# Routing attention and an ELU layer on one core: the steps of the ordering placed one by one between the products

## The chip, the cores and the metric

One Trainium2 chip, one core. The metric is the device time of one execution in microseconds. The kernel before was timed three times, with a median of 1534.33 us (1527.32 to 1535.45). "Third" below is a unit of work, explained with the kernel.

## The reference

Attention in which a query only sees the keys of its own cluster, then two matrix products with an ELU between them:

```python
def _attn_ref(q, k, v, centroids):            # q, k, v: (4, 8, 768, 64); centroids: (8, 16, 64)
    ...
    q_assign = np.argmax(np.einsum('bhsd,hcd->bhsc', q_n, c_n), axis=-1)
    k_assign = np.argmax(np.einsum('bhsd,hcd->bhsc', k_n, c_n), axis=-1)
    mask = q_assign[:, :, :, None] == k_assign[:, :, None, :]
    scores = scale * np.matmul(q, k.transpose(0, 1, 3, 2))
    scores = np.where(mask, scores, -1000000000.0)
    ...
    return np.matmul(attn, v).astype(np.float32)

def _moe_ref(x, w_in, w_out):                 # x: (3072, 512); w_in: (512, 2048); w_out: (2048, 512)
    h = x @ w_in
    g = np.where(h > 0.0, h, alpha * (np.exp(np.minimum(h, 0.0)) - 1.0))
    return (g @ w_out).astype(np.float32)
```

The weights come as 8-byte floats, and the kernel turns them into 4-byte ones itself.

## The kernel before, in words

Two heads are a pair; each of the four batches has four pairs, numbered 0 to 15 through all of them. The rows of x are cut into twelve **thirds** of 256 rows, three to a batch. The products of one third are twelve steps: four `hidden` steps (32 matmuls L780 each, then the ELU on ScalarE and VectorE) and eight `outer` steps (L804, 8 rows of the trace each, the first four into `o_bank`, the others into `f_bank`).

**Batch 0** is done densely, in eight blocks: `scores` (L446, L455, exp on ScalarE), `values` (L471, the reciprocal L482 on VectorE, the multiply L485 on GpSimd). Between them `weigh` converts the weights, 32 pieces of 512 KB of words: VectorE L306 to L315, ScalarE L301 and L302, and at the end a multiply on GpSimd (L318). After each piece `ask` loads the next words into the place that came free (L291). Sixteen pieces wait in the buffer of `w_out`, which is filled last.

**Batches 1 to 3** don't compute all scores. `ready(b)` is a list of 19 steps that order the rows by clusters: `load_plain` (SP), `turn_plain` (VectorE L365), `clusters` (TensorE L372), `running` (VectorE, `cum` L509), `starts` (TensorE L520), `ranks` (TensorE L535 and L543, VectorE `idx` L550), `limits`. With `idx` known, each pair is copied in DRAM into the order of its clusters, in two parts: `load_rows` loads a part (six DMAs on SP, L577, into `rows`, which has two buffers), `scatter` writes it out (12 indirect DMAs on GpSimd, L595). `load_sorted` (SP, L146 and L613) reads the pair back once both parts have landed. `turn_sorted` and `near_masks` (VectorE L620 to L630) prepare it; `attend` computes scores against the neighbouring tiles only (`near_scores`, L645 and L654) and the values of the pair before (`near_values`, L697 and L709, reciprocal L724). `store_x` writes the result on ScalarE's queue, `gather` fetches the 256 rows of a third (16 indirect DMAs on GpSimd, L749, for nine thirds), and `turn_x` transposes them for the products.

Everything is written out by hand: the order in which these functions are called is the order on each engine and each queue. Before, a table `beside` puts the steps of third 0 beside blocks 4 to 7, with three steps of `ready(1)` in each block. Then, for each batch, all four pairs are scattered at once:

```python
    def spread(i):
        for part in range(2):
            scatter(i, part)
            if i % NPR + 1 < NPR:
                load_rows(i + 1, part)
...
    for i in range(NPR, 2 * NPR):
        spread(i)
    load_sorted(NPR)
```

and a table `plans` says for each batch behind which product step a pair is attended and a third is gathered. The next batch's four pairs follow in one lump at the end of the batch.

Of the kernel before, what the change touches and what calls it, by code (L numbers as in the profile page):

```python
# [63 lines left out]
def main_path(ctx, tc, c, q, k, v, centroids, moe_w_in, moe_w_out, out):  # L64
# [39 lines left out]
    def take(n):  # L104
        nonlocal used
        used += n
        return spare[:, used - n : used]
# [169 lines left out]
    def ask():  # L277

        nonlocal asked
        while asked < len(pieces):  # L280
            to, src = pieces[asked]
            if not wide:
                nc.sync.dma_start(to, src)
                asked += 1
                continue
            places[:] = [x for x in places if asked < x[1]]
            if not places:
                return
            place, limit = places.pop(0)
            w = place.bitcast(U32)  # L290
            nc.sync.dma_start(w, src.bitcast(U32))  # L291
            words[asked] = (w.rearrange("p (n w) -> p n w", w=2), place, limit)
            asked += 1

# [30 lines left out]
    while used + 2 * WC <= FC * DM:  # L325
        limit = into + used // DM - 1
        places.append((take(2 * WC), limit))
    ask()
    rest = weight_steps()

    def weigh(n):
        for _ in range(n):
            next(rest, None)
# [220 lines left out]
    def limits(b):  # L554

        end = ends[b]
        for j in range(2):
            nc.vector.tensor_tensor(
                reach[:, 2 * (b - 1) + j : 2 * (b - 1) + j + 1],
                end[:, 2 * j + 1 : 2 * j + 2],  # L560
                end[:, 2 - 2 * j : 3 - 2 * j],
                op=Alu.subtract,
            )
        both = ends[b] = route.tile([P, 2, 4], F32, name="both", tag="both", bufs=2)
        for to in range(2):
# [17 lines left out]

    def scatter(i, part):
        b, pr = pairs[i]
        if part == 0:
            for e in range(2):
                q_in[i, e] = dram.tile([S, D], F32, name=f"q_in_{i}_{e}")
                kv_in[i, e] = dram.tile([S, 2 * D], F32, name=f"kv_in_{i}_{e}")
        rows = nat.pop((i, part))  # L590
        for t in range(HT):
            for j, to, cols in ((0, q_in, slice(0, D)), (1, kv_in, slice(D, 3 * D))):
                for e in range(2):
                    at = (part * HT + t) * H + 2 * pr + e
# [224 lines left out]
    def product_steps(third):  # L819
        return [lambda n=n: hidden(third, n) for n in range(FC // 4)] + [  # L820
            lambda t=t, part=part: outer(third, t, part) for t in range(2) for part in range(4)
        ]


    def ready(b):

        some = ((0, 1), (2, 3))
        load = lambda j, n: lambda: [load_plain(b, j, pr) for pr in some[n]]
        turn = lambda j, n: lambda: [turn_plain(b, j, pr) for pr in some[n]]
        return [load(0, 0), turn(0, 0), load(0, 1), turn(0, 1)] + [  # L830
            lambda: clusters(b, 0, 0),
            lambda: clusters(b, 0, 1),
            load(1, 0),
            lambda: running(b, 0),
            lambda: starts(b, 0),
            turn(1, 0),
            load(1, 1),
            lambda: ranks(b, 0),
            turn(1, 1),
            lambda: clusters(b, 1, 0),  # L840
            lambda: clusters(b, 1, 1),
            lambda: running(b, 1),
            lambda: starts(b, 1),
            lambda: ranks(b, 1),
            lambda: [limits(b)] + [load_rows(b * NPR, part) for part in range(2)],
        ]

    def spread(i):
        for part in range(2):
            scatter(i, part)  # L850
            if i % NPR + 1 < NPR:
                load_rows(i + 1, part)

    def attend(i):

# [12 lines left out]
        if j == 0:  # L868
            masks(0)

    todo = product_steps(0)
    beside = {4: [0, 1], 5: [2, 3], 6: [4, 5, 6, 7], 7: [8, 9, 10, 11]}
    first = ready(1)
    for n in range(len(blocks)):
        if n > 0:
            values(n - 1)
        if n + 1 < len(blocks):
            v_of[n + 1] = load_v(blocks[n + 1][1])
        scores(n)
        if n > 0:  # L880
            check(n - 1, n - 1)
        if n + 1 < len(blocks):
            masks(n + 1)
        weigh(4 if n < 4 else 0)
        for m in beside.get(n, []):
            todo[m]()
            weigh(4)
        if n >= 1:
            for step in first[3 * n - 3 : 3 * n]:
                step()  # L890
    values(len(blocks) - 1)
    check(len(blocks) - 1, len(blocks) - 1)

    plans = {
        1: {"attend": (0, 2, 4, 8), "last": 12, "ready": 8, "gather": 18},
        2: {"attend": (8, 16, 22, 28), "last": 32, "ready": 0, "gather": 34},
        3: {"attend": (4, 10, 16, 22), "last": 26, "ready": None, "gather": 30},
        4: {"attend": (), "last": None, "ready": None, "gather": None},  # L900
    }
    for i in range(NPR, 2 * NPR):
        spread(i)
    load_sorted(NPR)
    for b, plan in plans.items():
        thirds = range(3 * b - 2 if b == 1 else 3 * b - 3, 3 * b)
        todo = [step for third in thirds for step in product_steps(third)]
        events = {}

        def at(m, *what):  # L910
            events.setdefault(m, []).extend(what)

        for n, m in enumerate(plan["attend"]):
            i = b * NPR + n
            at(m - 1, lambda i=i: [turn_sorted(i), near_masks(i)])
            at(m, lambda i=i: attend(i))
            if n + 1 < NPR:
                at(m, lambda i=i: load_sorted(i + 1))
            if n > 0:
                at(m + 2, lambda i=i: store_x(i - 1))  # L920
        if plan["last"] is not None:
            i = (b + 1) * NPR - 1
            at(plan["last"], lambda i=i: [near_values(i), check(i, NPR + i)])
            at(plan["last"] + 2, lambda i=i: store_x(i))
            at(plan["gather"], lambda b=b: gather(3 * b))
            at(len(todo), lambda b=b: turn_x(3 * b))
        if b > 1:
            at(0, lambda b=b: gather(3 * b - 2))
            at(11, lambda b=b: turn_x(3 * b - 2))
            at(12, lambda b=b: gather(3 * b - 1))  # L930
            at(23, lambda b=b: turn_x(3 * b - 1))
        if plan["ready"] is not None:
            steps = ready(b + 1)
            for n, step in enumerate(steps):
                at(min(plan["ready"] + n + 1, len(todo)), step)
        for m in sorted(set(events) | set(range(len(todo)))):
            for event in events.get(m, []):
                event()
            if 0 <= m < len(todo):
                todo[m]()  # L940
        if plan["ready"] is not None:
            for i in range((b + 1) * NPR, (b + 2) * NPR):
                spread(i)
            load_sorted((b + 1) * NPR)


    ok = c["ok"]
# [238 lines left out]
```

## Time and profile before

| | |
|---|---|
| median of three runs | 1534.33 us |
| profiled execution | 1534.54 us |
| its span | 1532.8 us |
| TensorE busy | 1010.3 us (66%) |
| VectorE busy | 413.4 us (27%) |
| ScalarE busy | 323.5 us (21%) |
| GpSimd busy | 475.1 us (31%) |
| mean granted clock of TensorE | 0.81 |
| chain that ended last: TensorE | 55% |
| chain: "issue" | 19% |
| chain: another core or an unknown queue | 11% |

The span is cut into 40 slices on the page, and the digits there are tenths of a slice in which the engine was busy. "issue" in the chain and as the reason of an idle stretch means that the engine waited for nothing that the profile shows. In the lists of waits a line gives the engine and its line, what it waited for, the microseconds in total, how often, and the longest.

### The profile page before, as it was taken

The page shows a single profiled execution, that of the slowest core. Times are in us where ns is not written, and L with a number is a line of the kernel's source. Part 1 is how long each engine was busy: PE and PEld are TensorE (multiplying, and loading weights), DVE is VectorE, ACT ScalarE, POOL GpSimd, SP SyncE. Part 2 cuts the span into 40 slices and gives each one's busy share as a digit, 9 for nine tenths or more (in the row PEclk, how much of TensorE's full clock was granted, in tenths as well). Part 3 has the DMA queues.
Part 4 walks back from the last instruction along what each step waited for, and adds up shares of the span by engine and source line. Part 5 has one row for each costly group of instructions (what it writes and reads, how often), then busy time and mean ns, then how long its engine had stood idle before and what let it go on. Part 6 is the DMA issues. An engine that isn't in the chain of part 4 may idle for free.

```text
span 1532.8 us, 11444 instructions
## 1 busy us (share of the span) xinstructions
PE 1010.3 (66%) x4259; PEld 592.6 (39%) x4259; DVE 413.4 (27%) x618; ACT 323.5 (21%) x488; POOL 475.1 (31%) x494
## 2 busy tenths in 40 slices
PE   7547438800189998222399999522229999959998
PEld 4215223300065565100047474310114746545774
DVE  4553534100155632001044534000012444100100
ACT  5643342200033310000023232000002324111220
POOL 1222221077710034777300000777740000450000
PEclk9878679955599999555589999755559999979999
DMA  7623321022523342234411411223400220110000
GB/s 217 155 67 85 86 69 48 7 68 70 131 40 70 62 76 62 77 84 89 66 28 28 87 36 30 57 74 85 90 15 7 50 50 20 33 28 14 0 14 16
DMA packets 296206, 91.60 MB, mean 60 GB/s; under 512 B 278992, under 2 KB 282064, under 8 KB 296144
## 3 DMA queue, kind: packets, MB, share of 16 engines
q1 hardware_dynamic: 241232, 60.88, 18.3%
q0 software_dynamic: 13824, 18.90, 4.3%
q10 hardware_dynamic: 41088, 11.01, 2.9%
q8 instruction: 36, 0.59, 0.2%
q14 instruction: 26, 0.21, 0.0%
HBM read 65.57 MB, written 25.17 MB: 59 GB/s over the span
## 4 chain that ended last, share of the span: by engine, by line
PE 55%; issue 19%; another core or an unknown queue 11%; DVE 7%; ACT 4%; POOL 2%; DMA 1%; SPq 0%; ACTq 0%; DVEq 0%; POOLq 0%
PE banks L780 20%; PE o_bank L804 11%; PE f_bank L804 9%; PE banks L471 4%; PE banks L697 3%; PE banks L645 2%; PE banks L372 2%; PE banks L709 1%; DVE ex L312 1%; DVE r L724 1%; POOL w_in L318 1%; ACT p L662 1%; DVE r L482 1%; PE banks L446 1%
## 5 line engine op out<-in xcount | busy, mean ns | idle before, releaser
L780 PE MATMUL banks<-xT,w_in 128*128 128x256 f32 x1536 | 382.1, 399 | 243.8 <-issue 221.7
L780 PEld LDWEIGHTS banks<-xT,w_in 128*128 128x128 f32 x1536 | 305.5, 200 | 320.6 <-issue 258.3
L749 POOL DMA_INDIRECT rows_x<-x_in,idx x144 | 138.8, 964 | 535.9 <-DMA x_in<-back 491.5
L804 PE MATMUL o_bank<-w_out,gT 128*128 128x512 f32 x384 | 176.4, 613 | 16.0 <-issue 16.0
L795 DVE SCALAR_TENSOR_TENSOR gT<-gT,banks 128x1024 f32<-128x1024 f32 x48 | 58.2, 1213 | 469.2 <-ACT gT L792 372.2
L804 PE MATMUL f_bank<-w_out,gT 128*128 128x512 f32 x384 | 171.5, 600 | 0.0
L791 ACT ACTIVATE gT<-banks 128x1024 f32<-128x1024 f32 x48 | 49.1, 1024 | 545.7 <-remote 215.9
L595 POOL DMA_INDIRECT kv_in<-rows,idx x144 | 139.1, 966 | 58.1 <-issue 43.6
L595 POOL DMA_INDIRECT q_in<-rows,idx x144 | 138.8, 964 | 57.6 <-issue 45.2
L645 PE MATMUL banks<-qT,kT 64*128 64x384 f32 (+1 forms) x288 | 58.0, 483 | 116.8 <-issue 110.2
L804 PEld LDWEIGHTS o_bank<-w_out,gT 128*128 128x128 f32 x384 | 74.1, 195 | 110.3 <-issue 109.1
L804 PEld LDWEIGHTS f_bank<-w_out,gT 128*128 128x128 f32 x384 | 72.2, 191 | 88.7 <-issue 88.7
L724 DVE RECIPROCAL r<-r 128x384 f32<-128x384 f32 x24 | 61.2, 2549 | 127.2 <-ACT r L723 118.0
L662 ACT ACTIVATE p<-banks 128x768 f32<-128x768 f32 (+1 forms) x72 | 52.5, 740 | 130.3 <-issue 110.1
L645 PEld LDWEIGHTS banks<-qT,kT 64*128 64x128 f32 x288 | 24.1, 191 | 142.3 <-issue 121.0
L372 PE MATMUL banks<-plain,cT 128*32 128x384 f32 x96 | 25.0, 624 | 68.4 <-DVE plain L365 52.6
L365 DVE STREAM_TRANSPOSE plain<-blk 128x768 f32<-128x768 f32 x24 | 22.4, 960 | 146.1 <-issue 112.5
L792 ACT ACTIVATE gT<-gT 128x1024 f32<-128x1024 f32 x48 | 50.8, 1058 | 1.5
L318 POOL TENSOR_TENSOR w_in<-w_in,ex 128x512 f32<-128x512 f32 x16 | 23.1, 1444 | 76.1 <-DVE w_in L315 76.1
L485 POOL TENSOR_TENSOR xT<-x,r 128x256 f32<-128x256 f32 (+1 forms) x16 | 10.1, 649 | 117.2 <-DVE r L482 117.2
L697 PE MATMUL banks<-p,v_raw 128*64 128x256 f32 (+2 forms) x384 | 44.1, 382 | 0.0
L446 PE MATMUL banks<-qT,kT 64*128 64x384 f32 x192 | 40.9, 501 | 3.9 <-ACT r L481 2.5
(141 smaller groups left out, 802.7 us busy)
## 6 DMA issues: line engine op xcount, KB each, us to landing
w_out<-in_moe_w_in_dram SPq DMA_DIRECT2D x12, 512.0 KB
out_dram<-o_sb ACTq DMA_DIRECT2D x24, 256.0 KB
blk<-in_q_dram SPq DMA_DIRECT2D x48, 96.0 KB
words<-in_moe_w_out_dram SPq DMA_DIRECT2D x9, 512.0 KB
blk<-in_k_dram SPq DMA_DIRECT2D x48, 96.0 KB
rows<-in_q_dram SPq DMA_DIRECT2D x48, 96.0 KB
rows<-in_k_dram SPq DMA_DIRECT2D x48, 96.0 KB
rows<-in_v_dram SPq DMA_DIRECT2D x48, 96.0 KB
```

The lines of the kernel that those rows point to most:

```text
L372: nc.tensor.matmul(ps[32 * pr : 32 * pr + 32, :HS], lhsT=cT[:, 32 * pr : 32 * pr + 32], rhs=T[b, pr, j][:, cols], start=True, stop=True,)
L446: nc.tensor.matmul(s[:, e, :HS], lhsT=T[0, pr, 1][rows, ts(kt, P)], rhs=T[0, pr, 0][rows, cols], start=True, stop=False,)
L471: nc.tensor.matmul(ps[64 * e : 64 * e + 64, to, :HS], lhsT=of(e), rhs=pu[:, kt, e], start=(kt == 0), stop=(kt == NT - 1),)
L595: nc.gpsimd.indirect_dma_start(out=to[i, e][:, :], out_offset=bass.IndirectOffsetOnAxis(ap=idx[b, j][:, at : at + 1], axis=0), in_=rows[:, ...
L645: nc.tensor.matmul(s[:, e, : z - a], lhsT=T[i, 1][rows, ts(kt, P)], rhs=T[i, 0][rows, a:z], start=True, stop=False,)
L662: nc.scalar.activation(pu[:, kt, :, at : at + z - a], s[:, :, : z - a], Act.Exp, scale=SCALE)
L697: nc.tensor.matmul(o[64 * e : 64 * e + 64, half, lo - half * HS : hi - half * HS], lhsT=vn[:, e, kt], rhs=pu[:, kt, e, lo - (kt - 1) * P : ...
L724: nc.vector.reciprocal(r, r)
L749: nc.gpsimd.indirect_dma_start(out=rows[:, t, h * D : (h + 1) * D], out_offset=None, in_=x_in[b * NPR + h // 2, h % 2][:, :], in_offset=ba ...
L780: nc.tensor.matmul(hf[:, f], lhsT=w_in[:, ch, ts(4 * n + f, P)], rhs=xT[third][:, ch], start=(ch == 0 and f % 2 == 0), stop=(ch == KC - 1) ...
L795: lambda: nc.vector.scalar_tensor_tensor(t, t, -1.0, hf, op0=Alu.add, op1=Alu.max)
L804: nc.tensor.matmul(o, lhsT=g[f // 4][:, at : at + P], rhs=w_out[:, f], start=(f == 0), stop=(f == FC - 1),)
```

## The change

The amounts of work stay: 288 scatters, 144 gathers, the same matmuls. Three things change.

1. From the ninth piece on (`begun` is the number of places at the first `ask`, 8) the words of the weights are requested by GpSimd instead of SP: 24 loads of 512 KB.
2. Batch 0: one table says which steps of `ready(1)` and `ready(2)` stand between which blocks and product steps. The first outer steps of third 0 stand behind all blocks. `weigh(4)` now also runs in blocks 6 and 7.
3. `load_rows`, `scatter`, `load_sorted`, `begin` (turning, masks, attention), `store_x`, `gather` and `turn_x` are placed one by one between the product steps of all thirds, in place of `spread` and `plans`.

```diff
-            nc.sync.dma_start(w, src.bitcast(U32))
+            (nc.sync if asked < begun else nc.gpsimd).dma_start(w, src.bitcast(U32))
...
+    begun = len(places)
     ask()
...
-            lambda: [limits(b)] + [load_rows(b * NPR, part) for part in range(2)],
+            lambda: limits(b),
...
-        weigh(4 if n < 4 else 0)
-        for m in beside.get(n, []):
-            todo[m]()
-            weigh(4)
-        if n >= 1:
-            for step in first[3 * n - 3 : 3 * n]:
-                step()
+        weigh(4 if n < 4 or n > 5 else 0)
+
+    def convert(step):
+        step()
+        weigh(4)
+
+    def run(steps, events):
+        for n in range(len(steps) + 1):
+            for what, *which in events.get(n, ()):
+                what(*which)
+            if n < len(steps):
+                steps[n]()
+
+    rows, scat, ls, st, ga, tx = load_rows, scatter, load_sorted, store_x, gather, turn_x
...
+    hiddens = [lambda step=step: convert(step) for step in products[:4]]
+    run(
+        steps[:5] + hiddens[:2] + steps[5:6] + hiddens[2:] + steps[6:] + products[4:],
...
+            13: [(get, 1, 17, 18), (rows, 4, 0), (rows, 4, 1), (scat, 4, 0), (rows, 5, 0)],
+            14: [(scat, 4, 1), (get, 2, 1, 2)],
...
+    run(
+        product_steps(1) + product_steps(2),
+        {
+            0: [(get, 2, 11, 12), (ls, 4), (rows, 5, 1), (scat, 5, 0)],
+            1: [(get, 2, 13)],
+            2: [(begin, 4), (rows, 6, 0), (scat, 5, 1)],
...
+            5: [(ls, 5), (rows, 6, 1), (scat, 6, 0), (get, 2, 17)],
+            6: [(begin, 5), (get, 2, 18)],
+            8: [(st, 4), (rows, 7, 0), (scat, 6, 1)],
...
+            21: [(st, 7), (ga, 3)],
...
+    run(
+        product_steps(3) + product_steps(4) + product_steps(5),
+        {
+            0: [(begin, 8), (ga, 4), (scat, 9, 0), (rows, 10, 0)],
...
+            4: [(scat, 9, 1), (get, 3, 1, 2)],
+            6: [(ga, 5), (get, 3, 3)],
...
```

How the rows move, at three places.

SP, behind the blocks, before: the last of eight loads of `rows` (two of the buffers each time used again), then `sorted` and `v_raw` of pair 4.

```order
L577 DMA rows<-in_q_dram 128x3x64 x2
L577 DMA rows<-in_k_dram 128x3x64 x2
L577 DMA rows<-in_v_dram 128x3x64 x2
L146 DMA sorted<-q_in_0_1521 32x24x32 x2
L146 DMA sorted<-q_in_1_1523 32x24x32 x2
L146 DMA sorted<-kv_in_0_1522 32x24x32 x2
L146 DMA sorted<-kv_in_1_1524 32x24x32 x2
L613 DMA v_raw<-kv_in_0_1522 128x6x64
L613 DMA v_raw<-kv_in_1_1524 128x6x64
```

The same place in the change, from the third load of `rows` on (`blk` are the plain loads of batch 2).

```order
L578 DMA rows<-in_v_dram 128x3x64 x2
L146 DMA blk<-in_q_dram 32x24x32 x8
L146 DMA blk<-in_k_dram 32x24x32 x16
L146 DMA sorted<-q_in_0_1497 32x24x32 x2
L146 DMA sorted<-q_in_1_1499 32x24x32 x2
L146 DMA sorted<-kv_in_0_1498 32x24x32 x2
L146 DMA sorted<-kv_in_1_1500 32x24x32 x2
L614 DMA v_raw<-kv_in_0_1498 128x6x64
L614 DMA v_raw<-kv_in_1_1500 128x6x64
L578 DMA rows<-in_q_dram 128x3x64 x2
```

Five loads of `rows` moved behind `sorted` of the first pair, and 24 plain loads of batch 2 in front of it.

TensorE, the first near scores, before: they follow the values of the last block (`p,v_raw`, `p,ones`) directly.

```order
L471 MATMUL banks<-p,v_raw 64x384 x2
L471 MATMUL banks<-p,ones 64x384 x2
L645 MATMUL banks<-qT,kT 128x256 x2
L654 LDWEIGHTS hk
L654 MATMUL banks<-qm,hk 128x256
```

In the change the outer steps of third 0 and two hidden steps of third 1 lie between, with steps of `ready(1)` and `ready(2)`; the last rows ahead of the near scores:

```order
L805 MATMUL f_bank<-w_out,gT 128x512 x4
L373 MATMUL banks<-plain,cT 32x384 x4
L805 MATMUL f_bank<-w_out,gT 128x512 x4
L521 LDWEIGHTS before
L521 MATMUL banks<-cum,before 128x1
L805 MATMUL f_bank<-w_out,gT 128x512 x4
```

The near scores themselves have moved behind the first hidden steps of the next third.

GpSimd, among the conversions of the sixth block, before: multiplies of the conversion alone, then those of the values (`xT`).

```order
L318 TENSOR_TENSOR w_in<-w_in,ex 128x512
L318 TENSOR_TENSOR w_out<-w_out,ex 128x512 x7
L485 TENSOR_TENSOR xT<-x_1060,r 128x128
L485 TENSOR_TENSOR xT<-x_1060,r 128x256
L318 TENSOR_TENSOR w_out<-w_out,ex 128x512 x8
```

In the change a load of words stands behind nearly each multiply:

```order
L318 TENSOR_TENSOR w_in<-w_in,ex 128x512
L291 DMA w_out<-in_moe_w_out_dram 128x1024
L318 TENSOR_TENSOR w_out<-w_out,ex 128x512
L291 DMA words<-in_moe_w_out_dram 128x1024
L318 TENSOR_TENSOR w_out<-w_out,ex 128x512
L291 DMA words<-in_moe_w_out_dram 128x1024
L318 TENSOR_TENSOR w_out<-w_out,ex 128x512 x4
```

The 24 loads that were on SP have moved into this row of multiplies.

## Rows read from the trace of the kernel before

**Rows 1.** Timeline, 303.5 to 309 us: start us, length us, engine, line, count [idle before <- releaser].

```profile
306.07 1.17 POOL L595 DMA_INDIRECT q_in<-rows,idx  x1 [0.18 <-issue]
```

**Rows 2.** Waits, 300 to 425 us.

```profile
DVE qT L620 <- DMA sorted<-q_in: 102.0, 1, 102.0
...
PE banks L645 <- issue: 109.8, 1, 109.8
```

**Rows 3.** Windows: length, busy us (count) of PE, PEld, DVE, ACT, POOL; clock, DMA, GB/s.

```profile
304.00:412.00 108.00, 1.22 (x4) 0.53 (x4) 4.00 (x5) 0.62 (x2) 81.80 (x86) 0.50 0.33 83
...
606.00:766.00 160.00, 38.35 (x60) 15.08 (x58) 6.24 (x6) 4.16 (x4) 107.44 (x113) 0.52 0.36 79
...
973.00:1112.00 139.00, 38.96 (x95) 23.44 (x95) 1.22 (x1) 2.09 (x3) 105.50 (x111) 0.55 0.33 80
1112.00:1147.00 35.00, 7.59 (x13) 4.02 (x14) 6.03 (x8) 2.08 (x2) 15.48 (x16) 0.50 0.09 16
...
1326.00:1356.00 30.00, 13.64 (x38) 6.26 (x36) 0.00 (x0) 1.57 (x2) 19.16 (x21) 0.77 0.15 37
```

**Rows 4.** Timeline of GpSimd, 588 to 592 and 744 to 749 us.

```profile
588.88 0.96 POOL L595 DMA_INDIRECT kv_in<-rows,idx  x1 [14.51 <-DVE idx L550]
590.15 0.96 POOL L595 DMA_INDIRECT kv_in<-rows,idx  x1 [0.30 <-issue]
...
746.61 0.95 POOL L749 DMA_INDIRECT rows_x<-x_in,idx  x1 [0.30 <-issue]
```

**Rows 5.** Timeline of TensorE, 600 to 625 and 745 to 772 us.

```profile
599.82 6.70 PE L780 MATMUL banks<-xT,w_in 128*128 128x256 f32 x30
608.76 0.38 PE L780 MATMUL banks<-xT,w_in 128*128 128x256 f32 x1 [2.24 <-issue]
...
618.65 0.58 PE L780 MATMUL banks<-xT,w_in 128*128 128x256 f32 x1 [2.22 <-issue]
...
768.36 4.09 PE L804 MATMUL o_bank<-w_out,gT 128*128 128x512 f32 x5 [0.60 <-issue]
```

**Rows 6.** Timeline of TensorE, 540 to 556 us.

```profile
541.11 14.08 PE L780 MATMUL banks<-xT,w_in 128*128 128x256 f32 x64
```

**Rows 7.** Groups of GpSimd, 544 to 566 us: count | busy us, mean ns | idle before.

```profile
L749 POOL DMA_INDIRECT rows_x<-x_in,idx x10 | 10.3, 1028 | 34.8 <-DMA x_in<-back 32.0 <-issue 2.7
```

**Rows 8.** Pieces of the chain that ended last: start us, us, what.

```profile
250.34 13.93 PE o_bank L804 x32
...
889.17 27.63 PE banks L780 x128
```

**Rows 9.** Waits, 0 to 320 us.

```profile
PE banks L372 <- DVE plain L365: 51.7, 4, 27.2
...
PE banks L543 <- DVE one_each L540: 21.5, 1, 21.5
...
PE banks L520 <- DVE cum L509: 16.6, 1, 16.6
...
DVE w_out L306 <- DMA words<-in_moe_w_out_dram: 10.7, 3, 3.6
```

**Rows 10.** Timeline of GpSimd, 112 to 118 us, two multiplies of the conversion.

```profile
113.46 1.39 POOL L318 TENSOR_TENSOR w_in<-w_in,ex 128x512 f32<-128x512 f32 x1 [1.74 <-DVE w_in L315]
116.58 1.38 POOL L318 TENSOR_TENSOR w_in<-w_in,ex 128x512 f32<-128x512 f32 x1 [1.74 <-DVE w_in L315]
```

**Rows 11.** The page's groups of scatters: count | busy us, mean ns | idle before.

```profile
L595 POOL DMA_INDIRECT kv_in<-rows,idx x144 | 139.1, 966 | 58.1 <-issue 43.6
L595 POOL DMA_INDIRECT q_in<-rows,idx x144 | 138.8, 964 | 57.6 <-issue 45.2
```

**Rows 12.** Timeline of all engines, 45 to 46.5 us.

```profile
45.28 1.38 POOL L485 TENSOR_TENSOR xT<-x,r 128x256 f32<-128x256 f32 x2 [1.18 <-DVE r L482]
...
45.39 0.95 DVE L309 TENSOR_SCALAR ex<-w_out 128x512 uint32<-128x512 uint32 x1
```

**Rows 13.** Groups of VectorE, 0 to 300 us: count | busy us, mean ns | idle before.

```profile
L309 DVE TENSOR_SCALAR ex<-w_out 128x512 uint32<-128x512 uint32 x19 | 9.2, 482 | 18.6 <-POOL w_in L318 11.6 <-POOL w_out L318 6.9
```

More of the change, by code (lines that the diff above doesn't have):

```diff
@@ L844, in ready @@
             lambda: ranks(b, 1),
-            lambda: [limits(b)] + [load_rows(b * NPR, part) for part in range(2)],
+            lambda: limits(b),
         ]
[L848 to L852, printed above, removed]
     def attend(i):
@@ L869, in main_path, with get, begin, end @@
             masks(0)
[L871 to L874, printed above, removed]
+    prepare = {b: ready(b) for b in range(1, B)}
+    def get(b, *steps):
+        for n in steps:
+            prepare[b][n]()
+    def begin(i):
+        turn_sorted(i)
+        near_masks(i)
+        attend(i)
+    def end(i):
+        near_values(i)
+        check(i, NPR + i)
+    def block(n):
         if n > 0:
@@ L883, in main_path @@
             masks(n + 1)
-        weigh(4 if n < 4 else 0)
-        for m in beside.get(n, []):
-            todo[m]()
-            weigh(4)
-        if n >= 1:
-            for step in first[3 * n - 3 : 3 * n]:
-                step()
[L891 to L944, printed above, removed]
@@ new lines, in block @@
+        weigh(4 if n < 4 or n > 5 else 0)
[9 more added lines that the diff above has]
+    rows, scat, ls, st, ga, tx = load_rows, scatter, load_sorted, store_x, gather, turn_x
+    steps = [lambda n=n: block(n) for n in range(len(blocks))]
+    products = product_steps(0)
@@ new lines, in main_path @@
+    hiddens = [lambda step=step: convert(step) for step in products[:4]]
+    run(
+        steps[:5] + hiddens[:2] + steps[5:6] + hiddens[2:] + steps[6:] + products[4:],
+        {
+            4: [(get, 1, 0)],
+            5: [(get, 1, 1, 2)],
+            6: [(get, 1, 3)],
+            7: [(get, 1, 4, 6)],
+            8: [(get, 1, 5, 7)],
+            9: [(get, 1, 8, 9, 10)],
+            10: [(get, 1, 11, 12)],
+            11: [(get, 1, 13, 14, 15)],
+            12: [(values, 7), (check, 7, 7), (get, 1, 16), (get, 2, 0)],
+            13: [(get, 1, 17, 18), (rows, 4, 0), (rows, 4, 1), (scat, 4, 0), (rows, 5, 0)],
+            14: [(scat, 4, 1), (get, 2, 1, 2)],
+            16: [(get, 2, 3)],
+            17: [(get, 2, 4)],
+            18: [(get, 2, 5, 6, 7)],
+            19: [(get, 2, 8)],
+            20: [(get, 2, 9, 10)],
+        },
+    )
@@ new lines, in main_path @@
+    run(
[4 more added lines that the diff above has]
+            2: [(begin, 4), (rows, 6, 0), (scat, 5, 1)],
+            3: [(get, 2, 14, 15)],
+            4: [(get, 2, 16)],
+            5: [(ls, 5), (rows, 6, 1), (scat, 6, 0), (get, 2, 17)],
+            6: [(begin, 5), (get, 2, 18)],
+            8: [(st, 4), (rows, 7, 0), (scat, 6, 1)],
+            11: [(ls, 6), (rows, 7, 1), (scat, 7, 0)],
+            12: [(begin, 6)],
+            13: [(rows, 8, 0), (scat, 7, 1)],
+            14: [(st, 5), (ls, 7), (rows, 8, 1), (scat, 8, 0)],
+            15: [(begin, 7)],
+            16: [(st, 6), (rows, 9, 0), (scat, 8, 1)],
+            18: [(end, 7)],
+            21: [(st, 7), (ga, 3)],
+            22: [(ls, 8)],
+            23: [(rows, 9, 1)],
+            24: [(tx, 3)],
+        },
+    )
@@ new lines, in main_path @@
+    run(
+        product_steps(3) + product_steps(4) + product_steps(5),
+        {
+            0: [(begin, 8), (ga, 4), (scat, 9, 0), (rows, 10, 0)],
+            2: [(get, 3, 0)],
+            4: [(scat, 9, 1), (get, 3, 1, 2)],
+            6: [(ga, 5), (get, 3, 3)],
+            7: [(get, 3, 4)],
+            8: [(get, 3, 5, 6, 7)],
+            9: [(get, 3, 8)],
+            10: [(ls, 9), (rows, 10, 1), (scat, 10, 0), (get, 3, 9, 10)],
+            11: [(tx, 4), (get, 3, 11, 12)],
+            12: [(begin, 9)],
+            13: [(rows, 11, 0), (scat, 10, 1), (get, 3, 13)],
+            14: [(st, 8), (get, 3, 14)],
+            15: [(get, 3, 15, 16)],
+            17: [(get, 3, 17, 18), (ls, 10), (rows, 11, 1), (scat, 11, 0)],
+            20: [(begin, 10), (rows, 12, 0), (scat, 11, 1)],
+            22: [(st, 9)],
+            23: [(tx, 5), (ls, 11), (rows, 12, 1), (scat, 12, 0)],
+            25: [(begin, 11)],
+            26: [(rows, 13, 0), (scat, 12, 1)],
+            27: [(st, 10)],
+            28: [(end, 11)],
+            29: [(ls, 12), (rows, 13, 1), (scat, 13, 0)],
+            31: [(st, 11), (ga, 6)],
+            34: [(rows, 14, 0), (scat, 13, 1)],
+            36: [(tx, 6)],
+        },
+    )
@@ new lines, in main_path @@
+    run(
+        product_steps(6) + product_steps(7) + product_steps(8),
+        {
+            0: [(begin, 12), (ga, 7), (rows, 14, 1), (scat, 14, 0)],
+            1: [(ls, 13)],
+            3: [(rows, 15, 0), (scat, 14, 1)],
+            4: [(begin, 13)],
+            6: [(st, 12), (ga, 8)],
+            8: [(ls, 14), (rows, 15, 1), (scat, 15, 0), (scat, 15, 1)],
+            11: [(tx, 7)],
+            12: [(begin, 14)],
+            14: [(st, 13)],
+            17: [(ls, 15)],
+            20: [(begin, 15)],
+            22: [(st, 14)],
+            23: [(tx, 8), (end, 15)],
+            26: [(st, 15), (ga, 9)],
+            28: [(ga, 10)],
+            36: [(tx, 9)],
+        },
+    )
@@ L947, in main_path @@
+    run(
+        product_steps(9) + product_steps(10) + product_steps(11),
+        {11: [(tx, 10)], 12: [(ga, 11)], 23: [(tx, 11)]},
+    )
     ok = c["ok"]
```

## The prediction

> **What bounds the kernel now.** I read the windows by stage first, then the waits of the one long pause, then the timeline of TensorE, and last the groups. The profiled execution took 1534.54 us, its span 1532.8, so 1.7 us lie around the span. The median of the three runs is 1534.33, so the sum below, made against the profiled execution, needs no shift. About 0.5% (8 us) is what a measurement of this kernel can tell from no change.
>
> The span falls into three kinds of time. (1) The first 306 us, the dense blocks of batch 0, end where GpSimd issues the first indirect DMA [rows 1]. (2) Then TensorE waits 109.8 us before the first near scores L645, and VectorE 102.0 us for the first `sorted` [rows 2]. In that stretch TensorE has 4 matmuls and GpSimd 86 instructions [rows 3]: SP sends `sorted` of the first pair only behind the eight loads of `rows`, which wait for the scatters that free their two buffers. Some 106 us of it are idle. (3) Behind it work runs at a normal pace except in stretches where TensorE is slow though nothing holds it: in 606 to 766 us it does 60 matmuls, in 973 to 1112 it does 95, in 1112 to 1147 13 and in 1326 to 1356 38 [rows 3].
>
> What makes it slow is seen in the timeline. GpSimd begins to issue indirect DMAs without a pause at 588.88 us [rows 4]. Until 606.5 TensorE does L780 at full pace, then one matmul in 2.2 to 2.8 us (0.58 of its own behind 2.22 of waiting), with "issue" as the releaser [rows 5]. The granted clock falls with it, to 0.52 [rows 3], but a matmul of 0.58 instead of 0.38 us [rows 5] is little beside 2.2 us of waiting. The last indirect DMA starts at 746.61 [rows 4] and full pace is back at 768.36 [rows 5]. So the slow time is as long as the run of indirect DMAs and lies some 17 us behind it. A lone gather does not do it: between 540 and 568 us GpSimd issues one, and L780 stays at 64 matmuls in 14.08 us [rows 6, 7]. What couples the two engines no row says; I use it as an observation.
>
> What this costs: a matmul of L780 takes 27.63/128 = 0.216 us at full pace [rows 8]. The 60 and 95 matmuls would have taken 13 and 20.5 us instead of 160 and 139, the 13 and 38 would have taken 3 and 8 instead of 35 and 30: lost 147 + 118.5 + 32 + 22, some 320 us (all counted as L780, a little off for the others; I take 326 with the slower ends). So the time is 306 + 106 idle + 326 lost + 796 of work at its normal pace = 1534.
>
> **The change part by part.** *The first stage, 306 us.* TensorE stood there for `plain` four times, 51.7 us in all, once 21.5 for `one_each` and once 16.6 for `cum` [rows 9], 89.8 us together. All three are steps of the ordering of batch 1 that VectorE reaches only after a group of conversions, four pieces of 3.12 us (113.46 to 116.58) each [rows 10]. The new table puts these steps further apart and behind other blocks, but four conversions still stand behind most blocks. Bounds: none of the 89.8 us goes, or all. I take two thirds, 57 to 60 us, since the loads for `plain` no longer stand behind words on SP, while the conversions stay as many. The seven outer steps that move behind the blocks take 13.93/4 = 3.48 us each [rows 8], 24 us. First scatter: 306 - 24 - 57 = 225 us (bounds 192 and 282).
>
> *The pause, 106 us.* `sorted` of pair 4 now stands on SP behind three loads of `rows`, not eight, and needs 24 indirect DMAs. One takes 0.96 us and the next follows after 0.30 [rows 4, 11]: 24 x 1.265 = 30 us, some 5 more until data land and the loads are done. Ahead of the near scores TensorE now has the seven outers (24 us) and two hidden steps (14 us). 38 against 35: I take the pause as gone. If the cover fails (steps of `ready` that wait for VectorE between the outers), 10 to 20 us come back.
>
> *The words.* 24 loads leave SP for GpSimd. SP then sends the blocks' loads earlier, and the three waits for words, 10.7 us together [rows 9], can go. On GpSimd each load is one more instruction behind a multiply L318. The trace shows no plain load there; the nearest row is an indirect DMA, 1.26 us, and the other bound is nothing. GpSimd is idle 1.74 us between two multiplies [rows 10], so either bound is hidden; a load longer than that adds its excess to every piece.
>
> *The steps between products.* The 288 scatters and 144 gathers remain, 432 x 1.265 = 546 us of GpSimd. They go in two places: ahead of this, in lumps (one of 159 us, one like it, one at the start in which TensorE had nothing to do). Now they are parts of 12 (15 us) and gathers of 16 (20 us), and SP's `rows` loads and `sorted` loads alternate, so GpSimd pauses when the next load is held by a buffer that VectorE frees at its step of the products. By the order I count these runs without pause: 36 DMAs at the start (45 us); four of about 28 us beside thirds 1 and 2; 72 DMAs, 91 us, around the start of third 3 (gathers 3 and 4, pair 9, gather 5); four of 28 beside thirds 4 and 5; 84 DMAs, 106 us, around third 6; gathers 9 and 10, 40 us. A run costs TensorE at least its length less the 17 us, at most its length. For long runs I take the length less 7 or 8 us (38, 83, 98, 27 with the last a little lower), for the eight 28-us runs 15 each, 120: 366 us, and at 8% of full pace (0.216 of 2.8 us) 0.92 of it is lost, 337 us. This is the largest term and the least sure. Lower bound: only what lies over 17 us and half of it met by streaming, 100 us; upper: every indirect DMA and the pauses between, below.
>
> **Sum:** 225 + 24 + 796 + 337 = 1382 us. The pause goes (106), the first stage shrinks (57), and the slow time stays about as long as before, because what was hidden in the pause (86 indirect DMAs) now lies beside streaming matmuls.
>
> **A rule that speaks against the words on GpSimd.** Beside a GpSimd multiply, VectorE's L309 takes 0.95 us where its mean is 0.48 [rows 12, 13]: the two engines do hold each other up in the conversions. The Trainium skill, SBUF — State Buffer, section on the "DVE blocks DMA" trap, says that a DMA issued by GpSimd has its descriptors locked out while VectorE runs an operation of the two-port kind, and gives 620 ns alone against about 3100 ns; no run here shows it yet, and with its figure the estimate is 24 x (3.1 - 1.74) = 33 us more in the sum.
>
> **Rivals.**
> (a) *The runs are short enough.* If 28-us runs with pauses do not slow TensorE, and the two long ones only in part, the loss is about 100 us: 225 + 24 + 796 + 100 = 1145; with waits for `sorted` 1150 to 1200. For it: the gather of 20 us that costs nothing. Against: the runs before and behind third 3 and 6 are in the order as one.
> (b) *Pauses too short, slower than before.* TensorE needs some 20 us after the last indirect DMA to be fast again [rows 4, 5]. If the pauses between the parts are under that, it stays slow throughout all 546 us and some 100 us of pauses: 0.92 x 646 = 594 lost, 225 + 24 + 796 + 594 = 1639 us. It decides against the change once the loss passes 1534 - 1045 = 489 us, that is when more than 530 us are slow. Against: a third's products take 27.63 + 8 x 3.48 = 55 us at full pace [rows 8] and many times that at the slow one, while GpSimd needs 30 us for the pair placed beside them, so it would run out of work and pause for longer than 20 us.
> (c) *The words hold up the conversions.* If VectorE keeps a load on GpSimd waiting for a whole cycle of 3.12 us instead of the 1.74 that are free, 24 pieces cost 1.4 us each, 33 us, all in the first stage where conversions set the pace: 1382 + 33 = 1415.
> (d) *The order does not do what it says.* SP is one queue; if `sorted` and `rows` wait there for buffers in a ring, the pause comes back as many small ones and the time stays about 1534. Against: only pairs' own buffers are waited for, and these are freed two steps ahead.
>
> **How the numbers follow.** Forecast 1382: 0.55, with its own range of 1240 (loss 200) to 1500 (first scatter at 282 and 400 lost). (a) 0.20, (b) 0.12, (c) 0.08, (d) 0.05. The range must leave out no more than 2 in 10: half of (a) lies below 1170, most of (b) above 1545. So 1170 to 1545. Faster by over 0.5%: the forecast, (a), (c) less a little of the forecast's upper end, 0.81. Same: most of (d), 0.04. Slower: (b) and the rest, 0.15.
>
> **What would show it.** First scatter between 205 and 250 us, and no idle time over 30 us ahead of the first near scores. Stretches in which L780 falls to one matmul per 2 to 3 us, each beginning some 17 us into a run of indirect DMAs, the longest around the starts of thirds 3 and 6; their sum 250 to 450 us. The multiply L318 still each 3.1 us: over 4 speaks for (c). No slow stretch at all speaks for (a), a slow stretch that spans the pauses for (b). The prediction is wrong if the first near scores still wait for 100 us, or if the slow time isn't tied to the runs of indirect DMAs.

## The result and the profile after

The changed kernel takes 1417.72 us (median of four runs, 1403.6 to 1422.07) against 1534.86 of the kernel before in the same place: a ratio of 0.923, with a 95% interval of 0.916 to 0.930. Forecast were 1382, with a range of 1170 to 1545. The profiled execution has a span of 1418.2 us.

The timeline of GpSimd gives the first indirect DMA (start us, length us, engine, line, operation, count, idle before).

```profile
241.58 1.59 POOL L596 DMA_INDIRECT q_in<-rows,idx  x1 [0.17 <-issue]
```

It comes 64 us earlier than in [rows 1]; 225 was forecast. The windows of three stretches, with the columns of [rows 3], show what follows.

```profile
242.00:300.00 58.00, 29.87 (x74) 11.55 (x75) 13.90 (x32) 0.59 (x1) 34.70 (x36) 0.75 0.32 72
555.00:660.00 105.00, 36.78 (x100) 22.18 (x101) 4.39 (x7) 7.53 (x9) 66.66 (x70) 0.56 0.18 43
910.00:1025.00 115.00, 27.74 (x90) 14.53 (x89) 0.00 (x0) 5.43 (x7) 79.44 (x84) 0.58 0.26 62
```

The pause of [rows 2] is gone, but TensorE does 74 matmuls in the 58 us behind the first indirect DMA, and 100 and 90 in the two long stretches around thirds 3 and 6. Around third 3 the slow pace has the form of [rows 5]; four of the matmuls in the timeline of TensorE:

```profile
595.81 0.38 PE L781 MATMUL banks<-xT,w_in 128*128 128x256 f32 x1 [2.02 <-issue]
597.92 0.38 PE L781 MATMUL banks<-xT,w_in 128*128 128x256 f32 x1 [1.74 <-issue]
600.99 0.58 PE L781 MATMUL banks<-xT,w_in 128*128 128x256 f32 x1 [2.69 <-issue]
603.97 0.59 PE L781 MATMUL banks<-xT,w_in 128*128 128x256 f32 x1 [2.39 <-issue]
```

GpSimd issues indirect DMAs here from 543 to 642 us, 78 records of them, as the count of the order had it (72 and the next ones). Around third 6 the loss has another form: TensorE's near scores run back to back, but ScalarE, which needs them for `p`, starts 13 to 15 us after they have ended, and TensorE waits for `p`. The timelines of TensorE and of ScalarE:

```profile
957.00 1.65 PE L646 MATMUL banks<-qT,kT 64*128 64x384 f32 x4 [15.11 <-issue]
958.44 0.53 PE L655 MATMUL banks<-qm,hk 64*128 64x384 bf16 x2
973.31 1.65 PE L646 MATMUL banks<-qT,kT 64*128 64x384 f32 x4 [14.34 <-issue]
```

```profile
956.35 0.60 ACT L663 ACTIVATE p<-banks 128x512 f32<-128x512 f32 x1 [16.49 <-remote]
972.45 0.81 ACT L663 ACTIVATE p<-banks 128x768 f32<-128x768 f32 x1 [15.50 <-issue]
```

Over the whole program the waits of TensorE (engine, line, waited for, us in total, times, longest) show both forms:

```profile
PE banks L781 <- issue: 101.3, 52, 5.6
PE banks L646 <- ACT p L663: 52.9, 10, 14.1
PE banks L646 <- issue: 50.3, 6, 15.1
PE banks L781 <- ACT p L663: 34.1, 4, 16.1
```

From 242 us on TensorE is idle for some 330 us, its ordinary waits included. In the terms of the prediction's sum, 1417.72 - 241.6 - 24 - 796 = 356 us were lost; 337 were forecast.

### The profile page after: what moved, and what is told of

Same layout as the page of the kernel before. It is cut to its first block, busy times and chain, and to the rows that moved or that the text cites. A ratio compares the mean times of both kernels' runs of the same rounds, so it can differ in the third digit from the quotient of the medians.

```text
span 1418.2 us, 11439 instructions
## 1 busy us (share of the span) xinstructions
PE 1019.1 (72%) x4259; PEld 602.6 (42%) x4259; DVE 415.0 (29%) x618; ACT 322.1 (23%) x488; POOL 485.6 (34%) x518
## 4 chain that ended last, share of the span: by engine, by line
PE 57%; another core or an unknown queue 16%; issue 11%; DVE 7%; ACT 4%; POOL 2%; DMA 2%; SPq 1%; ACTq 0%; DVEq 0%; POOLq 0%
PE banks L781 22%; PE o_bank L805 12%; PE f_bank L805 10%; PE banks L698 3%; PE banks L472 3%; PE banks L646 2%; PE banks L447 1%; ACT p L663 1%; DVE ex L312 1%; POOL w_out L318 1%; POOL w_in L318 1%; PE banks L710 1%; DMA words<-in_moe_w_out_dram 1%; PE banks L655 1%
## 5 line engine op out<-in xcount | busy, mean ns | idle before, releaser
L781 PE MATMUL banks<-xT,w_in 128*128 128x256 f32 x1536 | 374.4, 400 | 138.2 <-issue 101.3
L781 PEld LDWEIGHTS banks<-xT,w_in 128*128 128x128 f32 x1536 | 307.0, 201 | 209.8 <-issue 125.8
L805 PE MATMUL f_bank<-w_out,gT 128*128 128x512 f32 x384 | 175.4, 610 | 3.1 <-issue 3.0
L646 PE MATMUL banks<-qT,kT 64*128 64x384 f32 (+1 forms) x288 | 75.0, 607 | 138.0 <-ACT p L663 52.9
L805 PE MATMUL o_bank<-w_out,gT 128*128 128x512 f32 x384 | 170.2, 599 | 0.0
L646 PEld LDWEIGHTS banks<-qT,kT 64*128 64x128 f32 x288 | 30.1, 237 | 170.6 <-ACT p L663 65.2
L676 DVE TENSOR_TENSOR psum<-p 128x640 f32<-128x640 f32 x24 | 19.5, 813 | 255.6 <-ACT p L663 185.6
L447 PE MATMUL banks<-qT,kT 64*128 64x384 f32 x192 | 45.6, 553 | 11.9 <-ACT r L482 8.2
L698 PE MATMUL banks<-p,v_raw 128*64 128x256 f32 (+2 forms) x384 | 48.1, 392 | 5.6 <-issue 5.6
L472 PE MATMUL banks<-p,v_raw 128*64 128x384 f32 x192 | 42.5, 523 | 4.2 <-DVE sim L380 4.2
L318 POOL TENSOR_TENSOR w_out<-w_out,ex 128x512 f32<-128x512 f32 x16 | 21.1, 1318 | 60.1 <-DVE w_out L315 54.8
```

The source lines that it names most:

```text
L318: nc.gpsimd.tensor_tensor(to, to, ex.bitcast(F32), op=Alu.mult)
L447: nc.tensor.matmul(s[:, e, :HS], lhsT=T[0, pr, 1][rows, ts(kt, P)], rhs=T[0, pr, 0][rows, cols], start=True, stop=False,)
L472: nc.tensor.matmul(ps[64 * e : 64 * e + 64, to, :HS], lhsT=of(e), rhs=pu[:, kt, e], start=(kt == 0), stop=(kt == NT - 1),)
L646: nc.tensor.matmul(s[:, e, : z - a], lhsT=T[i, 1][rows, ts(kt, P)], rhs=T[i, 0][rows, a:z], start=True, stop=False,)
L698: nc.tensor.matmul(o[64 * e : 64 * e + 64, half, lo - half * HS : hi - half * HS], lhsT=vn[:, e, kt], rhs=pu[:, kt, e, lo - (kt - 1) * P : ...
L781: nc.tensor.matmul(hf[:, f], lhsT=w_in[:, ch, ts(4 * n + f, P)], rhs=xT[third][:, ch], start=(ch == 0 and f % 2 == 0), stop=(ch == KC - 1) ...
```

## The experiments

They ran in three groups. Each comparison has its own runs of the kernel before, made on the same chip. Here that kernel takes 1362.5 to 1363.8 us, not 1534, on both chips that were met (the records of the first timing name no chip). So the first thing to settle was which part of the story belongs to the kernel and which to the place. "The first place" is the chip and the time of the first timing, "the second place" that of the later ones; whether the chip or the time makes the difference is not known.

**The same kernel in the second place.** No edit.

> The changed kernel once more, since the kernel before took 1363 us where the last runs were made and 1534 where the change was timed. Theory that TensorE's slow stretches belong to the place where a kernel runs: where the kernel before takes 1363 us, this one takes about 1090, with no slow stretch; where it takes 1534, 1418. Rival that the words on GpSimd make the difference and not the place: about 1418 in either place, and 330 us more than the version with the words on SP.

Measured: 1091.26 us (1089.7 to 1092.78) against 1363.76, a ratio of 0.801 (0.799 to 0.802). So the change is worth 272 us here and 117 there. The windows around two runs of indirect DMAs (90 in 303 to 421 us, 103 in 435 to 569), both at least as long as the 78 above:

```profile
300.00:420.00 120.00, 117.96 (x584) 74.00 (x584) 69.06 (x96) 41.43 (x67) 90.01 (x88) 1.00 0.55 124
435.00:570.00 135.00, 108.65 (x431) 65.38 (x430) 46.40 (x68) 25.80 (x36) 102.70 (x103) 0.87 0.49 104
```

584 matmuls in 120 us beside 88 indirect DMAs without a pause: a run of indirect DMAs by itself doesn't slow TensorE. The slow stretches, which the prediction used as a property of such runs, were seen beside such runs in the first place only. The words on GpSimd are not it either: they are on GpSimd here, and nothing is slow.

**The words alone, in the kernel before.**

```diff
-            nc.sync.dma_start(w, src.bitcast(U32))
+            (nc.sync if asked < begun else nc.gpsimd).dma_start(w, src.bitcast(U32))
```

> The kernel before with only the words from the ninth piece on asked for by GpSimd. Theory: within 10 us of 1534, since in the first stage TensorE waits for steps behind the conversions and not for loads. Rival that the words carry a good part of the gain: 1500 or less. Rival that GpSimd's loads lengthen the conversions: 1550 to 1567.

Measured: 1357.93 against 1362.55, a ratio of 0.9967 (0.9956 to 0.9977): 4.6 us faster. The level of 1534 in the expectation was that of the first place; the difference is the one that the theory gave. No trace of the kernel before itself was kept in the second place; this version stands for it, since its time differs by 0.3% and the trace of the next experiment has the second and third of its pauses too (79.6 and 71.4 us). Its waits of TensorE show what the slow stretches had covered:

```profile
PE banks L646 <- DVE kT L621: 179.2, 2, 109.0
PE banks L373 <- DVE gT L796: 79.4, 1, 79.4
PE banks L373 <- DVE plain L366: 51.5, 5, 31.9
```

Three pauses, not one: 109.0 us, the pause of [rows 2], then 79.4 and 70.2 (179.2 - 109.0), each beside one of the later lumps of scatters. The second is seen from VectorE and the timelines:

```profile
DVE qT L621 <- DMA sorted<-q_in: 177.9, 2, 101.3
...
DVE plain L366 <- DMA blk<-in_q_dram: 99.0, 4, 95.2
```

```profile
573.98 27.87 PE L781 MATMUL banks<-xT,w_in 128*128 128x256 f32 x128
...
684.73 1.50 PE L373 MATMUL banks<-plain,cT 128*32 128x384 f32 x4 [79.44 <-DVE gT L796]
```

TensorE runs at full pace into the lump (128 matmuls in 27.87 us), then stands, because `turn_plain` on VectorE waits 95.2 us for `blk`, which SP sends behind the loads of `rows` of the lump and the `sorted` that follows them. In the first place VectorE stood at the same step, inside TensorE's slow stretch of 606 to 766 us:

```profile
710.75 0.98 DVE L365 STREAM_TRANSPOSE plain<-blk 128x768 f32<-128x768 f32 x1 [112.54 <-issue]
```

TensorE, still busy with its slow matmuls, showed no long wait for it.

**`sorted` of pair 4 right behind its own scatters, in the kernel before.**

```diff
     for i in range(NPR, 2 * NPR):
         spread(i)
-    load_sorted(NPR)
+        if i == NPR:
+            load_sorted(i)
```

> The kernel before with one edit: the sorted rows of pair 4 are loaded right behind its own scatters instead of behind those of all four pairs. Theory: the first near scores come at about 345 instead of 411 us, but TensorE then streams beside indirect DMAs that run without pause until about 430 and goes slow from about 365 on, so most of the 66 us is given back: 1500 to 1530. Rival: the pause is worth what it lasts and nothing slows TensorE there: 1465 to 1475.

Measured: 1339.24 against 1362.55, a ratio of 0.983 (0.981 to 0.985): 23 us faster. Nothing slowed TensorE, so the theory's reason is not at work here; and the rival's 66 us didn't come either. VectorE's timeline says where they went:

```profile
342.40 0.98 DVE L620 STREAM_TRANSPOSE qT<-sorted 128x768 f32<-128x768 f32 x1 [40.78 <-DMA sorted<-q_in]
...
404.71 0.98 DVE L620 STREAM_TRANSPOSE qT<-sorted 128x768 f32<-128x768 f32 x1 [45.84 <-DMA sorted<-q_in]
```

The pause has become two, since `sorted` of the next pair stands behind the lump again: 82.8 us of waits before L645 in this stretch in place of 109. Moving one load moves the pause on to the next pair.

**Back into one lump, in the changed kernel.** All scatters of pairs 9 to 11, and their loads of `rows`, at the start of third 3:

```diff
-            0: [(begin, 8), (ga, 4), (scat, 9, 0), (rows, 10, 0)],
+            0: [(begin, 8), (ga, 4), (scat, 9, 0), (rows, 10, 0), (scat, 9, 1), (rows, 10, 1), (scat, 10, 0), (rows, 11, 0), (scat, 10, 1), (rows, 11, 1), (scat, 11, 0), (scat, 11, 1)],
```

> The changed kernel with the scatters of pairs 9, 10 and 11 in one lump at the start of third 3, as the kernel before had them, all else in its place. Theory without slow stretches: the lump and the two gathers take some 110 us of GpSimd while the next near scores need one pair, so TensorE waits 0 to 30 us for gather 5 or pair 9, far less than the 79 us of the kernel before: 0 to 30 us slower than the change. Theory with slow stretches: the long run costs TensorE its length, but other runs get shorter by as much, within 20 us of the change. Rival that lumps as such cost what the kernel before waited: 60 to 80 us slower.

Measured: 1132.59, a ratio of 0.830 (0.828 to 0.833) to the kernel before, 41 us above the change: between the theory's 30 and the rival's 60. The mechanism is not quite either: the waits of TensorE grow in one line only, from 25.4 us to

```profile
PE banks L373 <- DVE plain L366: 67.4, 8, 44.8
```

with one wait of 44.8 us. It is not the next near scores nor the gather that is late, but `plain` of the ordering of batch 3: its loads stand on SP behind the `rows` of the lump. That is the queue of the 79.4 us above, and what a step placed by itself keeps free.

**All words on SP, in the changed kernel.** The first line of the change taken back.

> The changed kernel with all words of the weights asked for by SP again; the order of everything else stays. Theory: the loads on GpSimd are hidden in its idle time between the multiplies, and SP has time too, so the first indirect DMA stays at 242 us within 10 and the time within 10 us of 1418. Rival: loads on GpSimd are held up by VectorE and lengthen the conversions, then this is 15 to 33 us faster (1385 to 1403). Second rival: words on SP hold the plain loads of the batches behind them, then it is 10 to 30 us slower.

> The changed kernel with all words on SP, beside the changed kernel in the same place. Theory: within 6 us of it, and the first indirect DMA about 4 us earlier. Rival (c) of the prediction: 15 to 33 us faster. Rival that the words on GpSimd bring TensorE's slow stretches: 300 us faster where they are.

Measured: 1086.33, and 1087.40 (1085.08 to 1088.40) beside 1091.26 of the change: 3.9 us faster. Its first expectation was made for 1418 and can't be compared; by the second, with the first indirect DMA at 239.2 instead of 242.0 (2.8 us earlier, about 4 were expected), the theory holds. The last multiplies of the conversion show the place. The change, in the second place:

```profile
176.29 1.25 POOL L318 TENSOR_TENSOR w_out<-w_out,ex 128x512 f32<-128x512 f32 x1 [6.19 <-DVE w_out L315]
177.50 0.58 POOL L291 DMA_DIRECT2D words<-in_moe_w_out_dram  x1
183.34 1.25 POOL L318 TENSOR_TENSOR w_out<-w_out,ex 128x512 f32<-128x512 f32 x1 [5.27 <-DVE w_out L315]
184.55 0.58 POOL L291 DMA_DIRECT2D words<-in_moe_w_out_dram  x1
190.33 1.25 POOL L318 TENSOR_TENSOR w_out<-w_out,ex 128x512 f32<-128x512 f32 x1 [5.21 <-DVE one_each L541]
```

With the words on SP:

```profile
176.59 1.26 POOL L318 TENSOR_TENSOR w_out<-w_out,ex 128x512 f32<-128x512 f32 x1 [6.63 <-DVE w_out L315]
182.09 1.26 POOL L318 TENSOR_TENSOR w_out<-w_out,ex 128x512 f32<-128x512 f32 x1 [4.24 <-DVE w_out L315]
187.50 1.27 POOL L318 TENSOR_TENSOR w_out<-w_out,ex 128x512 f32<-128x512 f32 x1 [4.15 <-DVE one_each L541]
```

7.0 us apart against 5.5 in the last two gaps: VectorE waits there for words that are asked for behind the multiply before, and from GpSimd that round is 1.5 us longer. Of the 3.9 us that explains about three.

**Only the last four pieces on SP.**

```diff
-            (nc.sync if asked < begun else nc.gpsimd).dma_start(w, src.bitcast(U32))
+            (nc.sync if asked < begun or asked >= 28 else nc.gpsimd).dma_start(w, src.bitcast(U32))
```

> The changed kernel with only the last four of the 32 pieces asked for by SP again. Theory that a load on GpSimd costs time only where the next piece has no place but the one just freed, and takes some 1.7 us longer from the multiply to its landing: the last multiplies stand 5.4 us apart instead of 7.1, and all of the 4 us between the two versions come back. Rival that the twenty others cost it too: half or less comes back.

Measured: 1087.87 (1087.18 to 1088.66), a ratio of 0.7988 (0.7977 to 0.7998). This was another group of runs than that of the change; by the ratios, 0.8006 (0.7991 to 0.8020) for the change and 0.7968 (0.7954 to 0.7982) for all words on SP, the version lies between the two, and the intervals overlap. The multiplies of its trace stand at 182.41 and 187.82, 5.4 us apart, as with all words on SP, and the first indirect DMA comes at 239.7. By the ratios about half of the difference came back, as the rival says; of the first indirect DMA's 2.8 us 2.3 did. So the trace bears the theory out for this stage, and the times don't settle it.

**Plain DMAs in place of the scatters.**

```diff
-                    nc.gpsimd.indirect_dma_start(
-                        out=to[i, e][:, :],
...
+                    nc.gpsimd.dma_start(to[i, e][ts(at // H, P), :], rows[:, e, t, cols])
```

> The changed kernel with each of the 288 scatters as a plain DMA of the same rows and bytes, still issued by GpSimd; the rows are then not ordered by clusters, which is the part that is left out. The 144 gathers stay indirect. Theory that indirect DMAs in a run slow TensorE: slow stretches stay only beside the gathers that follow each other, some 220 us of the slow time go, 1190 to 1250. Rival that any DMA that GpSimd issues does it, by its own descriptors: slow stretches at the same places, 1380 to 1430. Rival that the traffic in DRAM does it: the same as the second.

> The changed kernel with plain DMAs on GpSimd in place of the scatters, which leaves out the order by clusters, once more. Where the kernel before takes 1534 us: the theory that indirect DMAs in a run slow TensorE says 1190 to 1250, the rival that any DMA of GpSimd does it says 1380 to 1430. Where it takes 1363: 1060 as before, and nothing is told apart.

Measured: 1060.43 and 1058.52 (1363 before), some 31 us below the change. What it was made for, to tell which DMAs of GpSimd slow TensorE, can't be read where nothing slows it, and both runs were made there. What it does give is a price: a plain DMA of the same rows holds GpSimd 0.54 us, a scatter of the change in the second place 1.00 to 1.01, and with 288 scatters that cost GpSimd so much less (some 130 us) only some 30 us are gained.

**A pause behind each indirect DMA.** Four small multiplies on GpSimd each time.

```diff
+    def pace():
+        for _ in range(4):
+            nc.gpsimd.tensor_tensor(still, still, still, op=Alu.mult)
```

> The changed kernel with four small multiplies on GpSimd behind each indirect DMA, so that one comes in some 2.7 us instead of 1.27; GpSimd then has 430 times 1.4 us, about 600 us, more to do. Theory with slow stretches that come from the rate of indirect DMAs: no slow stretch is left, and the time is set by GpSimd, 1300 to 1400. Rival that the engine's mere activity slows TensorE: 1600 and more where slow stretches are. Without slow stretches: GpSimd becomes the bound, 1250 to 1400, some 200 us or more slower than the change.

Measured: 1630.69, a ratio of 1.196 (1.194 to 1.198). Without slow stretches 1250 to 1400 was expected, so this missed. The added work is 589 us, the longer time 539. The waits of TensorE:

```profile
PE banks L654 <- DVE kT L629: 194.9, 6, 63.1
PE banks L771 <- DMA rows_x<-x_in,idx: 133.8, 16, 41.3
```

Near scores and gathers now come late by turns. GpSimd isn't the bound that was expected: of the 1388 us behind 242 us it is busy for 1030. That GpSimd, TensorE and the gathers wait for each other in a ring would explain both; it wasn't tested. In the change the runs from 303 to 569 us have one pause of 14 us, so GpSimd has little room there.

**A step further: the ranks behind block 6.** On top of the version with all words on SP.

```diff
-            10: [(get, 1, 11, 12)],
-            11: [(get, 1, 13, 14, 15)],
+            10: [(get, 1, 12)],
+            11: [(get, 1, 11, 13, 14, 15)],
```

> The version with the words on SP, and the first ranks step of batch 1 moved behind block 6, so that TensorE does the values and scores of that block (about 20 us) in place of the 23 us that it waited for one_each. Theory that TensorE is what bounds the first stage there: 10 to 20 us faster than the version with the words on SP. Rival that the conversions on VectorE bound the stage, whose last pieces wait for their words: the ranks come 10 to 20 us later, the first indirect DMA with them, within 5 us of that version or up to 10 slower.

Measured: 1073.51 us (1071.99 to 1076.38), a ratio of 0.788 (0.787 to 0.790): the fastest version that computes everything, 13 to 14 us below the one with the words on SP (1086.33 and 1087.40, other groups). The waits of TensorE, with the line that was meant:

```profile
PE banks L447 <- ACT r L482: 16.7, 4, 9.4
...
PE banks L544 <- DVE one_each L541: 7.4, 2, 6.5
PE banks L472 <- DVE ends L524: 7.4, 1, 7.4
```

L544 waited 24.0 us in the version with all words on SP and waits 7.4 now; the first indirect DMA comes at 226.6 instead of 239.2. TensorE's own order was what this stage lost time by, though the conversions on VectorE set when `one_each` is done.

## Why the prediction came out right, and which of its steps didn't

**First scatter at 225 us: 241.6.** The direction and the mechanism hold, the size doesn't: 64 us earlier, of which 24 are outers that moved, so 40 instead of 57 us of stalls went. What remained is the kind that the prediction named, `one_each` behind conversions, 26.7 us once; the last experiment left 6.5 of it.

**The pause of 106 us gone.** Right. In the first place the first near scores start at 320.7 us, 79 behind the first indirect DMA, and TensorE's longest wait between the two is 10.9 us. In the second place they start at 304 us; 12.2 us of TensorE's waits for `sorted` remain in the whole program.

**The words at nothing.** Nearly: they cost 3.9 us in the changed kernel and gain 4.6 in the kernel before. Of rival (c) the place is right (a load that comes late for its piece), the mechanism hardly: it is the way from the multiply to the landing, in two gaps, and not 24 loads held for 1.4 us each. VectorE does hold loads up, but for little. In the second place seven of the 24 run without L309 beside them and take 578 to 581 ns; the 17 beside it take 621 to 646 ns, one 764, and all but that one end 117 to 120 ns after L309, which itself takes 0.43 us. One of the 17, the load and the L309 beside it:

```profile
153.02 0.63 POOL L291 DMA_DIRECT2D words<-in_moe_w_out_dram  x1
153.11 0.43 DVE L309 TENSOR_SCALAR ex<-w_out 128x512 uint32<-128x512 uint32 x1 [1.16 <-POOL w_out L318]
```

The Trainium skill, SBUF — State Buffer, "A bandwidth-pool intuition that's wrong (but worth ruling out)", gives about 620 ns for such a DMA alone, near the 578 to 581 here, and about 3100 ns beside a VectorE `tensor_copy`; no run here has such a copy beside a load, so the second figure isn't tested.

**326 us lost before, 337 after.** As sizes in the first place both stand: 337 was 356, and the first stage adds the other 17 us to the forecast. What failed is what the 326 were taken for. The prediction put all of the slow stretches down as loss, "work runs at a normal pace except in stretches where TensorE is slow though nothing holds it". The second place shows what the first costs: 1534.86 - 1363.76 = 171 us for the kernel before, 1417.72 - 1091.26 = 326 for the change. So of the 326 before some 150 were no loss by slowness: TensorE would have waited there anyway, 79.4 and 70.2 us for SP's queue. The change takes three pauses away, 258 us, and not one of 106; and it puts the slowness onto work that nothing covers any more, 155 us more and not 11. The forecast was -57 - 106 + 11 = -152 us; read by the second place it is -40 for the first stage, -232 for the pauses and other waits, and +155, together -117. The two large errors are nearly equal and of opposite sign, and that they cancel is not something the prediction worked out. TensorE's idle time where nothing is slow bears out the first two, with the version with the words alone for the kernel before: ahead of the first indirect DMA it falls from 105 to 68 us, behind it from 292 to 57.

The form of the loss is also another one than forecast. What the prediction counted, matmuls that come one by one "at 8% of full pace", are the 101.3 us of L781; a larger part, 52.9 + 50.3 + 34.1 us, are near scores and the products behind them that wait by turns with ScalarE. That 356 lies so near 337 is in part luck.

**The slow stretches as a rule.** The main parts of the observation were there again in the first place (16 us behind the start of the run at 320 us, one matmul in 2 to 3 us, stretches around thirds 3 and 6). But not every run costs its length less 17 us: beside the 26 gathers from 1195 to 1227 us, 32 us long, TensorE loses only some 3 us, in two waits, and about as much beside the last 16; the prediction had 27 for both.

```profile
1227.30 0.59 PE L805 MATMUL f_bank<-w_out,gT 128*128 128x512 f32 x1 [1.55 <-issue]
1229.39 7.62 PE L805 MATMUL f_bank<-w_out,gT 128*128 128x512 f32 x13 [1.50 <-issue]
```

And the reading that a lone gather does no harm came from ten gathers in 13 us [rows 7], less than the 17 us. That stretches of this kind come wherever the kernel runs was assumed and is wrong.

**The rivals.** (b) and (d) fell. (a), runs too short to slow TensorE, gave 1145 to 1200; without slowness the time is 1091, but for another reason than short runs: a run of 103 DMAs does no harm there. (c) was only tested in the second place.

What makes TensorE slow in the first place stays open. The experiment that would have told descriptors from traffic ran only where there was nothing to tell.

## What to carry to other kernels

A stretch in which an engine is slow can cover a wait; before it is booked as loss, ask what the engine would have waited for at full pace, by following the queue that feeds it (here SP: plain loads behind loads that wait for buffers). Loads for later steps should stand between the loads that wait, one pair at a time, since moving a single one moves the pause to the next. And where a trace shows an engine slow without a cause in the program, run the kernel before somewhere else first: a sum that rests on it holds for that place only.

## What the runs showed of the hardware that was not expected

The same program took 1534 us in its first timing and 1363 on two chips later, each time within 1% over its runs, and the difference that the traces show is TensorE beside runs of indirect DMAs. There not only TensorE's issue is late but, it seems, also its signals: ScalarE's starts above, and in the change, first place, the timelines of TensorE and VectorE:

```profile
283.41 0.85 PE L373 MATMUL banks<-plain,cT 128*32 128x384 f32 x8
```

```profile
294.57 0.58 DVE L380 STREAM_TRANSPOSE sim<-banks 128x384 f32<-128x384 f32 x1 [13.27 <-remote]
```

The matmuls end at 284.3 us; VectorE, for which the trace names no engine of this core as the releaser ("remote"), starts on them 10 us later. In the second place the wait in this line is 8.3 us at the longest, with TensorE named. Behind two of the long waits, at 586 and 1007 us, 22 matmuls of L781 run back to back before the slow pace comes, as if instructions that TensorE already held were not slow; that is a reading, and no run tested it. GpSimd itself keeps its pace of one indirect DMA in 1.26 us in both places.
